# An attention stage whose probabilities and values stay in fp32: one fp32 product in place of three fp16 ones

## The chip, the cores and the metric

The kernel runs on one core of a Trainium2 chip. The metric is the time of one execution on the device in microseconds, the median of several runs. The engines named below are TensorE (PE, with its weight loads as PEld), VectorE (DVE), ScalarE (ACT), GpSimd (POOL) and SyncE (SP), which here issues DMAs.

## The reference, cut to what matters

Three stages follow each other: an attention with a forgetting bias, a mixture of eight experts whose gate is normalised by eight Sinkhorn rounds, and a bilinear layer. The change lies in the attention's last lines.

```
B, H, S, D = 2, 8, 576, 64
scores = q @ k.T / sqrt(D) + min(-(cum[:, None] - cum[None, :]), 0)   # causal
scores = scores - max(scores, -1)
attn = exp(scores)
attn = attn / (sum(attn, -1) + 1e-9)
x = attn @ v                                  # to (1152, 512)
x = sum over e of P[:, e] * (relu(x @ w1[e]) @ w2[e])    # E = 8
out = ((x @ w_a) * (x @ w_b)) @ w_out
```

## The kernel before, in words

The matmuls take fp16, and a matrix that needs more digits is split in two: hi is the fp16 rounding of the scaled fp32 value, lo the fp16 rounding of what hi left out. A product of two such matrices is three fp16 products, hi·hi, hi·lo and lo·hi, summed in fp32 in PSUM.

**Values.** `v_prep(b)` loads one batch of v (five blocks of 128 rows, the last of 64) into a staging buffer, takes a sum of squares on ACT for a power of two as scale, and splits each block into `vs[b]`: hi by ACT or POOL (L358, L362), lo by DVE or POOL (L372, L366 and L367). Each head has 64 hi columns, a column of ones whose product gives the row sum of the probabilities, and 64 lo columns. The staging buffers are `wun` for batch 0 and `stage` for batch 1, which also hold expert 0's weights.

**Probabilities.** The 1152 rows are nine tiles: four of 128 query rows for each batch, and a ninth with the last 64 rows of both. For each tile `row_max` makes scores and reduces them on DVE (`mxr`), `shift` brings the maxima into the transposed queries (`ush`, `ut`), and `probs` makes transposed scores in groups of up to 512 columns in PSUM (`st`). For each group ACT takes the exponential into an fp32 tile `p32` (L894), hi is copied to fp16 into `pt` by ACT, POOL or DVE (L901, L900), and lo is subtracted by POOL or DVE (L904, L903). When all key blocks of a head are there, `pv` multiplies: three matmuls for each key block (L922, L923, L924), with the probabilities as stationary operand, so that each loads 128 query columns (64 in the ninth tile) and streams 65 or 64 columns of values into `xp`. Over both batches these are 160 products of 128 query columns and 80 of 64. `x_tile` divides by the row sum (`rs`, `xb`, L936 to L938), splits the result and transposes it by DMA into `xt`.

**The rest.** Right behind each tile of attention comes expert 0 for that tile (`e0_tile`: gate, h as `mb<-xt,wun`, y as `mb<-wun,h`, with the relu and its split as `h` on ACT and DVE). Its PE instructions stand between those of the attention. After the ninth tile the attention's memory is given back, and experts 1 to 7 and the bilinear layer follow.

**The order of work.** Each instruction is recorded with the engines that could do it, an assumed cost, what it reads and writes, and a rank. A planner lays out the whole program before anything runs: it picks an engine for each instruction and an order for each engine, from the assumed costs. On the chip each engine then takes its instructions strictly in that order. So a change of a cost or of an instruction moves the order on all engines. The three fp16 matmuls of a product are assumed at 93 ns.

Of the kernel before, what the change touches and what calls it, by code (L numbers as in the profile page):

```python
# [246 lines left out]
def forgetting_attention_moe_bilinear_kernel(  # L247
# [14 lines left out]
    nc = tc.nc  # L262
# [110 lines left out]


    XE = 6
    NJ = S // 128
    att = ExitStack()
    ap = att.enter_context(tc.tile_pool(name="att", bufs=1))
# [1 line left out]
    NSS, NST, NP32, NPT, NB3 = 2, 2, 2, 5, 2  # L380
    ka1 = ap.tile([128, H, NT], F16, name="ka1")
    ka2 = ap.tile([128, H, NT], F16, name="ka2")
    vs = [ap.tile([128, NBLK, H, 130], F16, name=f"vs{b}") for b in range(B)]
    kn1 = ap.tile([128, H, 2, D], F16, name="kn1")
    kn2 = ap.tile([128, H, 2, D], F16, name="kn2")
    qa = [ap.tile([128, H, 2, D], F16, name=f"qa{i}") for i in range(2)]
# [2 lines left out]
    b4 = [ap.tile([128, H, 128], F16, name=f"b4_{i}") for i in range(2)]  # L389
    p32 = [ap.tile([128, 512], F32, name=f"p32_{i}") for i in range(NP32)]  # L390
    pts = [ap.tile([128, 2, 512], F16, name=f"pt{i}") for i in range(NPT)]
    xb = ap.tile([128, H, D], F32, name="xb")
    xhl = ap.tile([128, 2, DM], F16, name="xhl")
    raw = ap.tile([128, 6, DM], F32, name="raw")
# [77 lines left out]
    for x, key in ((kn2, ("kn2", 1)), (qa[0], ("qa", 0, 1)), (qa[1], ("qa", 1, 1))):  # L472
        g.add("POOL", 500, lambda x=x: nc.gpsimd.memset(x[:, :, 1], 0.0), w=[key], rank=0.5)
    for b in range(B):
        g.add("POOL", 200, lambda b=b: nc.gpsimd.memset(vs[b][:, :, :, 64:66], 1.0), w=[("vone", b)], rank=0.7)

    def consts_():
        f = sel.rearrange("p h a -> p (h a)")
# [105 lines left out]


    def v_prep(b, rank, rel=0.0):
        if b == 0:
            uf = [units[2 + i].rearrange("p z c f -> p (z c f)").bitcast(F32) for i in range(2)]
            sv = [uf[j // 4][:, (j % 4) * DM:(j % 4 + 1) * DM] for j in range(NBLK)]
            svk = [[("u", 2 + j // 4, (j % 4) // 2, 2 * (j % 2) + y) for y in range(2)] for j in range(NBLK)]  # L590
        else:
            sv = [stage[j // 4][:, (j % 4) * DM:(j % 4 + 1) * DM] for j in range(NBLK)]
            svk = [[("st", j // 4, j % 4)] for j in range(NBLK)]
        mxs = scol(NBLK)
        g.add("DVE", 60, lambda: nc.vector.memset(mxs, 0.0), w=[("vm", b)], rank=0)
        for j in range(NBLK):
            kr = 128 if j < NJ else vrem
            g.add("DMA", 1456 * kr / 128, lambda q, j=j, kr=kr: q.dma_start(
                out=sv[j][0:kr].rearrange("p (h d) -> p h d", h=H),
                in_=v[b, :, j * 128:j * 128 + kr, :].rearrange("h s d -> s h d")), w=svk[j], rank=rank, rel=rel)  # L600
            g.add("ACT", 800, lambda j=j, kr=kr: sumsq(mxs[0:kr, j:j + 1], sv[j][0:kr], junk[0:kr]), r=svk[j] + [("vm", b)], w=[("vmx", b, j)], rank=rank)
        sx, iv = scale_chain(mxs, 13, True, rank, [("vmx", b, j) for j in range(NBLK)], ("vsx", b), root=True)

        def svs():
            nc.vector.tensor_scalar(isx[:, b * NJ:(b + 1) * NJ], iv.to_broadcast([128, NJ]), 2.0 ** (13 - XE), None, op0=ALU.mult)
            nc.vector.tensor_scalar(isx[64 * b:64 * b + 64, 2 * NJ:2 * NJ + 1], iv[64 * b:64 * b + 64], 2.0 ** (13 - XE), None, op0=ALU.mult)

# [26 lines left out]
    def cc(ci, i, r=slice(0, 128)):  # L634
        return cst[r, ci, i:i + 1]
# [215 lines left out]

    stc, ptc, p3c = [0], [0], [0]

    def probs(t, zb, rank):

        z4 = t % 2
# [13 lines left out]
        for gr in groups:  # L870
# [8 lines left out]
            def mm(gr=gr, y=y, bb=bb):  # L879
                for w, (_, h, i) in enumerate(gr):  # L880
# [10 lines left out]
            nl = sum(i == (j if t < 2 * NJ else NJ) for (_, _, i) in gr)  # L891
            g.add("PE", (2 * len(gr) + nl) * pe_n(wd), mm, r=[("b3", zb), ("b4", z4), "idb", "msk"] + [("ka", nm, x) for nm in ("kn1", "kn2") for x in kts],
                  w=[("st", y)], rank=rank)
            g.add("ACT", 280 + n * 0.833, lambda y=y, p3=p3, kr=kr, n=n, bb=bb: nc.scalar.activation(  # L894
                p32[p3][0:kr, 0:n], st[y][0:kr, 0:n], AF.Exp, scale=cc(bb, ESC, slice(0, kr))), r=[("st", y), ("cst", bb)], w=[("p32", p3)], rank=rank)
            hi = pts[pi][0:kr, 0, 0:n]
            lo = pts[pi][0:kr, 1, 0:n]
            src = p32[p3][0:kr, 0:n]
            g.add(("DVE", "POOL", "ACT"), (70 + 0.6 * n, 150 + n, 170 + n * 0.833), (lambda hi=hi, src=src: nc.vector.tensor_copy(hi, src),
                  lambda hi=hi, src=src: nc.gpsimd.tensor_copy(hi, src),  # L900
                  lambda hi=hi, src=src: nc.scalar.activation(hi, src, AF.Copy)), r=[("p32", p3)], w=[("pt", pi, 0)], rank=rank)  # L901
            g.add(("DVE", "POOL"), (130 + 1.04 * n, 150 + 2.2 * n), (
                lambda hi=hi, lo=lo, src=src: nc.vector.tensor_tensor(out=lo, in0=src, in1=hi, op=ALU.subtract),  # L903
                lambda hi=hi, lo=lo, src=src: nc.gpsimd.tensor_tensor(out=lo, in0=src, in1=hi, op=ALU.subtract)),  # L904
                r=[("p32", p3), ("pt", pi, 0)], w=[("pt", pi, 1)], rank=rank)
            for w, blk in enumerate(gr):
                where[blk] = (pi, w)
            for h in range(H):
                mine = [(bb, h, i) for i in (range(j + 1) if t < 2 * NJ else [NJ, *range(NJ)])]
                if (bb, h) in done or not all(x in where for x in mine):  # L910
                    continue
                done.add((bb, h))
                at = [(x[2],) + where[x] for x in mine]

                def pv(h=h, bb=bb, at=at):
                    q0 = 0 if t < 2 * NJ else 64 * bb
                    o = xp[h // 4][q0:q0 + wd, (h % 4) * 65:(h % 4) * 65 + 65]
                    for x, (i, pi_, w) in enumerate(at):
                        kw = kcol(bb, i)[1]
                        ph, pl = (pts[pi_][0:kw, y, w * wd:(w + 1) * wd] for y in range(2))  # L920
                        v1, vl = vs[bb][0:kw, i, h, 0:65], vs[bb][0:kw, i, h, 66:130]
                        nc.tensor.matmul(o, lhsT=ph, rhs=v1, start=(x == 0), stop=False)  # L922
                        nc.tensor.matmul(o[:, 0:64], lhsT=ph, rhs=vl, start=False, stop=False)  # L923
                        nc.tensor.matmul(o, lhsT=pl, rhs=v1, start=False, stop=(x == len(at) - 1))  # L924

                g.add("PE", 93 * len(at), pv, r=[("pt", pi_, y) for (_, pi_, _) in at for y in range(2)] + [("vone", bb)]
                      + [(nm, bb, i) for (i, _, _) in at for nm in ("vs", "vh")], w=[("xp", h // 4)], rank=rank + 1)

    def x_tile(t, rank):
        xf = xb.rearrange("p h d -> p (h d)")  # L930
        hf = xhl.rearrange("p z d -> p (z d)")
        for gg in range(2):
            def f(gg=gg):
                o = xp[gg][:, 0:260].rearrange("p (h d) -> p h d", d=65)
                r4 = rs[:, 4 * gg:4 * gg + 4]
                nc.vector.tensor_scalar(r4, o[:, :, 64], 1e-9 * PSC, 2.0 ** (13 - XE), op0=ALU.add, op1=ALU.mult)  # L936
                nc.vector.reciprocal(r4, r4)
                nc.vector.tensor_tensor(out=xb[:, 4 * gg:4 * gg + 4], in0=o[:, :, 0:64],  # L938
                                        in1=r4.rearrange("p (h o) -> p h o", o=1).to_broadcast([128, 4, D]), op=ALU.mult)

            g.add("DVE", 900, f, w=[("xp", gg), ("xb", gg)], rank=rank)
        xbk = [("xb", 0), ("xb", 1)]
        g.add(("ACT", "POOL", "DVE"), (600, 690, 380), (lambda: nc.scalar.activation(xhl[:, 0], xf, AF.Copy),
              lambda: nc.gpsimd.tensor_copy(xhl[:, 0], xf), lambda: nc.vector.tensor_copy(xhl[:, 0], xf)), r=xbk, w=[("xhl", 0)], rank=rank)
        g.add(("DVE", "POOL"), (663, 1280), (lambda: nc.vector.tensor_tensor(out=xhl[:, 1], in0=xf, in1=xhl[:, 0], op=ALU.subtract),
              lambda: nc.gpsimd.tensor_tensor(out=xhl[:, 1], in0=xf, in1=xhl[:, 0], op=ALU.subtract)), r=[("xhl", 0)], w=xbk + [("xhl", 1)], rank=rank)
        g.add("SP", 1600, lambda: nc.sync.dma_start_transpose(
            out=xt[:, :, :, xc[t]:xc[t] + 128].rearrange("p z c t -> p (z c) t"), in_=hf),
            r=[("xhl", 0), ("xhl", 1)], w=[("xt", t)] + (["ncum", "ntail", "sn"] if t == 0 else []), rank=rank - 5, issue=1300.0)
# [836 lines left out]
```

## Time and profile before

| | us |
|---|---|
| median of 3 runs (1058.57 to 1062.61) | 1058.78 |
| the profiled execution | 1059.17 |
| its span, first to last instruction | 1057.3 |
| PE busy, share of the span | 1008.0 (95%) |
| DVE busy | 720.3 (68%) |
| ACT busy | 517.4 (49%) |
| POOL busy | 156.2 (15%) |

The shares are means over stages that differ. The attention with expert 0 lasts until about 225 us of the span; POOL does nearly all its work there. Matmuls overlap, and the recorded time of one is longer than its distance to the next, so the pace of TensorE is read from the starts of the rows.

### The profile page before, as it was taken

How to read it: one execution, taken by the hardware profiler on the slowest of the kernel's cores; microseconds unless marked ns; L12 is line 12 of the kernel's file. 1: busy time of each engine (PE TensorE's matmuls, PEld its weight loads, DVE VectorE, ACT ScalarE, POOL GpSimd, SP SyncE). 2: the span in 40 equal slices, each digit the busy share in tenths (PEclk: the TensorE clock that was granted, in tenths of full speed). 3: DMA queues.
4: the chain of work that ended last, by engine and by line, in shares of the span. 5: the costliest groups of instructions: out<-in, count | busy, mean ns of one | idle time of the engine just before them, and what ended most of it. 6: DMA issues, size and time to landing. Idle time of an engine off the chain costs nothing.

```text
span 1057.3 us, 18899 instructions
## 1 busy us (share of the span) xinstructions
PE 1008.0 (95%) x7676; PEld 625.6 (59%) x7676; DVE 720.3 (68%) x1488; ACT 517.4 (49%) x970; POOL 156.2 (15%) x190
## 2 busy tenths in 40 slices
PE   1688999999999999999999999999999999999998
PEld 0577777866546745754774674575476464555445
DVE  7986865159975898795789889489768684434201
ACT  5786567346535635653672774455355354343100
POOL 4876755320000000000000000000000000000000
PEclk9989999999999999999999999999999999999999
DMA  9883751021123134423324340431443652300001
GB/s 243 166 201 80 163 79 25 2 75 56 41 80 120 41 122 158 160 81 120 120 81 153 131 155 40 158 122 40 160 160 144 184 121 80 127 34 1 20 31 40
DMA packets 123063, 108.75 MB, mean 103 GB/s; under 512 B 87632, under 2 KB 100176, under 8 KB 119136
## 3 DMA queue, kind: packets, MB, share of 16 engines
q1 hardware_dynamic: 121632, 106.74, 33.9%
q8 instruction: 60, 0.98, 0.4%
q10 hardware_dynamic: 1344, 0.81, 0.3%
q14 instruction: 27, 0.22, 0.1%
HBM read 75.29 MB, written 18.09 MB: 88 GB/s over the span
## 4 chain that ended last, share of the span: by engine, by line
PE 88%; DVE 6%; SPq 2%; DMA 1%; issue 1%; ACT 1%; POOL 1%; DVEq 0%; POOLq 0%; ACTq 0%
PE yb L1048 10%; PE yb L1049 10%; PE yb L1050 10%; PE yb L1400 4%; PE yb L1402 4%; PE yb L1401 4%; PE mb L1400 3%; PE mb L1402 3%; PE mb L1401 3%; PE yb L1656 2%; PE yb L1654 2%; PE yb L1655 2%; PE yb L1584 2%; PE yb L1586 2%; PE yb L1585 2%; PE mb L1584 1%
## 5 line engine op out<-in xcount | busy, mean ns | idle before, releaser
L1048 PE MATMUL yb<-wun,ht 128*128 128x512 f16 x504 | 191.0, 379 | 0.0
L1050 PE MATMUL yb<-wun,ht 128*128 128x512 f16 x504 | 191.0, 379 | 0.0
L1049 PE MATMUL yb<-wun,ht 128*128 128x512 f16 x504 | 191.0, 379 | 0.0
L372 DVE SCALAR_TENSOR_TENSOR wun<-stage,sc,wun 128x1024 f16<-128x1024 f32 (+1 forms) x65 | 78.9, 1236 | 11.6 <-ACT wun L358 11.5
L1050 PEld LDWEIGHTS <-ht 128*128 128x128 f16 x504 | 49.3, 98 | 59.5
L1400 PE MATMUL yb<-sx,wun 128*128 128x288 f16 x288 | 82.3, 286 | 2.0 <-DVE sc L343 1.1
L1458 DVE SCALAR_TENSOR_TENSOR acc<-yb,pe,acc 128x512 f32<-128x512 f32 x63 | 47.3, 750 | 53.7 <-PE yb L1050 52.7
L1049 PEld LDWEIGHTS <-ht 128*128 128x128 f16 x504 | 49.3, 98 | 57.7 <-issue 0.3
L1048 PEld LDWEIGHTS <-ht 128*128 128x128 f16 x504 | 49.3, 98 | 57.6
L1402 PE MATMUL yb<-sx,wun 128*128 128x288 f16 x288 | 82.4, 286 | 0.0
L1401 PE MATMUL yb<-sx,wun 128*128 128x288 f16 x288 | 82.3, 286 | 0.0
L1401 PEld LDWEIGHTS <-wun 128*128 128x128 f16 x672 | 65.7, 98 | 22.3 <-issue 4.0
L1400 PEld LDWEIGHTS <-wun 128*128 128x128 f16 x672 | 65.7, 98 | 18.4
L1402 PEld LDWEIGHTS <-wun 128*128 128x128 f16 x672 | 65.7, 98 | 16.6
L358 ACT ACTIVATE wun<-stage,sc 128x1024 f16<-128x1024 f32 (+1 forms) x60 | 60.9, 1040 | 28.3 <-PE yb L1050 14.0
L355 ACT ACTIVATE jk<-stage 128x1024 f16<-128x1024 f32 x52 | 54.7, 1052 | 35.8 <-DMA stage<-in_moe_w_dram 35.3
L904 POOL TENSOR_TENSOR pt<-p,pt 128x512 f16<-128x512 f32 (+1 forms) x48 | 57.1, 1192 | 31.7 <-ACT pt L901 22.6
L1410 ACT ACTIVATE ht<-yb 128x288 f16<-128x288 f32 x96 | 38.8, 406 | 40.7 <-PE yb L1402 40.1
L1400 PE MATMUL mb<-xt,wun 128*128 128x288 f16 x192 | 54.9, 286 | 0.0
L1401 PE MATMUL mb<-xt,wun 128*128 128x288 f16 x192 | 54.9, 286 | 0.0
L1402 PE MATMUL mb<-xt,wun 128*128 128x288 f16 x192 | 54.9, 286 | 0.0
L1411 DVE SCALAR_TENSOR_TENSOR ht<-yb,ht 128x288 f16<-128x288 f32 x96 | 43.0, 453 | 17.1 <-ACT ht L1410 16.7
(358 smaller groups left out, 2639.3 us busy)
## 6 DMA issues: line engine op xcount, KB each, us to landing
stage<-in_moe_w_dram SPq DMA_DIRECT2D x26, 1024.0 KB, 5.3
md<-wun SPq DMA_DIRECT2D x15, 1024.0 KB, 3.9
wun<-md SPq DMA_DIRECT2D x11, 1024.0 KB, 5.0
mr<-in_moe_w_a_dram SPq DMA_DIRECT2D x12, 512.0 KB, 5.8
mr<-in_moe_w_b_dram SPq DMA_DIRECT2D x12, 512.0 KB, 3.9
mr<-in_moe_w_out_dram SPq DMA_DIRECT2D x6, 1024.0 KB, 4.9
stage<-in_moe_w_dram SPq DMA_DIRECT2D x22, 256.0 KB, 4.0
stage<-md SPq DMA_DIRECT2D x4, 1024.0 KB, 4.8
```

What stands on the lines that cost most here:

```text
L355: nc.scalar.activation(out, src, AF.Square, accum_out=dst)
L358: nc.scalar.activation(hi, src, AF.Copy, scale=scale)
L372: eng.scalar_tensor_tensor(out=lo, in0=src, scalar=scale, in1=hi, op0=ALU.mult, op1=ALU.subtract)
L904: lambda hi=hi, lo=lo, src=src: nc.gpsimd.tensor_tensor(out=lo, in0=src, in1=hi, op=ALU.subtract)),
L1048: nc.tensor.matmul(pp, lhsT=hh, rhs=wh, start=(f == 0), stop=False)
L1049: nc.tensor.matmul(pp, lhsT=hh, rhs=wl, start=False, stop=False)
L1050: nc.tensor.matmul(pp, lhsT=hl, rhs=wh, start=False, stop=(f == KF - 1))
L1400: nc.tensor.matmul(p, lhsT=wh, rhs=xh, start=first and ch == 0, stop=False, skip_group_check=True)
L1401: nc.tensor.matmul(p, lhsT=wh, rhs=xl, start=False, stop=False, skip_group_check=True)
L1402: nc.tensor.matmul(p, lhsT=wl, rhs=xh, start=False, stop=ch == 1, skip_group_check=True)
L1411: g.add("DVE", 160 + 1.04 * CN, lambda: nc.vector.scalar_tensor_tensor(out=hl(), in0=src(), scalar=0.0, in1=hh(), op0=ALU.max, op1=ALU.sub ...
L1458: g.add("DVE", 663, lambda t=t, z=z: nc.vector.scalar_tensor_tensor(out=acc[:, t], in0=yb[z], scalar=pe[:, t, e:e + 1], in1=acc[:, t], op0 ...
```

## The change

Both batches are in `FV`, the list of batches whose probabilities and values stay in fp32. v is loaded straight into `vs[b]`, now an fp32 tile of 65 columns for each head (the 64 values and the ones); its splits are gone, and the sum of squares is kept, since its scale still sets that of the output. The exponential is written in fp32 straight into the memory of `pt` (`ptf` is that memory seen as fp32); the hi copy and the lo subtraction are gone. One fp32 matmul takes the place of three fp16 ones, with an assumed cost of 125 ns. The scale of v, which was multiplied into hi and lo, is now applied in `x_tile` through `isx`, and for the ninth tile through a new column `xs8` that is put together by one POOL memset and two small DVE copies.

```diff
+    FV = (0, 1)
-    vs = [ap.tile([128, NBLK, H, 130], F16, name=f"vs{b}") for b in range(B)]
+    vs = [ap.tile([128, NBLK, H, 65], F32, name=f"vs{b}") if b in FV else ap.tile([128, NBLK, H, 130], F16, name=f"vs{b}") for b in range(B)]
+    ptf = [x.rearrange("p z n -> p (z n)").bitcast(F32) for x in pts]
+    xs8 = scol()
...
     def v_prep(b, rank, rel=0.0):
-        if b == 0:
+        if b in FV:
+            sv = [vs[b][:, j, :, 0:64] for j in range(NBLK)]
+            svk = [[("vs", b, j)] for j in range(NBLK)]
+        elif b == 0:
...
+        if b in FV:
+            g.add("DVE", 70, lambda: nc.vector.tensor_copy(xs8[64 * b:64 * b + 64], isx[64 * b:64 * b + 64, 2 * NJ:2 * NJ + 1]),
+                  r=[("isx", b)], w=["xs8"], rank=rank + 0.6)
+            return
...
+            if bb in FV:
+                g.add("ACT", 280 + n * 0.833, lambda y=y, pi=pi, kr=kr, n=n, bb=bb: nc.scalar.activation(
+                    ptf[pi][0:kr, 0:n], st[y][0:kr, 0:n], AF.Exp, scale=cc(bb, ESC, slice(0, kr))),
+                    r=[("st", y), ("cst", bb)], w=[("pt", pi, 0), ("pt", pi, 1)], rank=rank)
+            else:
+                split_p(y, pi, p3, kr, n, bb, rank)
...
+                        if bb in FV:
+                            nc.tensor.matmul(o, lhsT=ptf[pi_][0:kw, w * wd:(w + 1) * wd], rhs=vs[bb][0:kw, i, h], start=(x == 0), stop=(x == len(at) - 1))
+                            continue
...
-                g.add("PE", 93 * len(at), pv, r=[("pt", pi_, y) for (_, pi_, _) in at for y in range(2)] + [("vone", bb)]
+                g.add("PE", (125 if bb in FV else 93) * len(at), pv, r=[("pt", pi_, y) for (_, pi_, _) in at for y in range(2)] + [("vone", bb)]
...
+        rsc = xs8 if t == 2 * NJ else isx[:, t:t + 1] if t // NJ in FV else 2.0 ** (13 - XE)
...
-                nc.vector.tensor_scalar(r4, o[:, :, 64], 1e-9 * PSC, 2.0 ** (13 - XE), op0=ALU.add, op1=ALU.mult)
+                nc.vector.tensor_scalar(r4, o[:, :, 64], 1e-9 * PSC, rsc, op0=ALU.add, op1=ALU.mult)
```

The first products of the first tile on PE, before: `xp` is the output, `vs` the values, `pt` the probabilities.

```order
L922 LDWEIGHTS pt_107
L922 MATMUL xp_136<-vs_94,pt_107 128x65
L923 LDWEIGHTS pt_107
L923 MATMUL xp_136<-vs_94,pt_107 128x64
L924 LDWEIGHTS pt_107
L924 MATMUL xp_136<-vs_94,pt_107 128x65
```

The same place now, with the two matmuls before it and the next tile's transpose behind it; an fp32 matmul stands here as one row, its weight loads within it.

```order
L912 LDWEIGHTS ka_92
L912 MATMUL st_135<-b_0_103,ka_92 128x128
L914 LDWEIGHTS idb
L914 MATMUL st_135<-msk_131,idb 128x128
L941 MATMUL xp_136<-vs_94,pt_107 128x65 x4
L941 MATMUL xp_137<-vs_94,pt_108 128x65 x4
L857 LDWEIGHTS ut_122
L857 MATMUL ss_133<-id_129,ut_122 128x128
```

All eight heads of the tile now stand together behind the last scores, and each has one matmul where it had three.

DVE before, from the second lo split of batch 0's values to the first tile's shift (`vs<-wun` are those splits, `mxr` the row maxima, `ush` and `ut` the shift).

```order
L372 SCALAR_TENSOR_TENSOR vs_94<-wun_77,sc,vs_94 128x8x64 x2
L521 TENSOR_REDUCE sc<-mb_84 1x1
L372 SCALAR_TENSOR_TENSOR vs_94<-wun_78,sc,vs_94 64x8x64
L795 TENSOR_REDUCE mxr<-ss_132 128x4
L795 TENSOR_REDUCE mxr<-ss_133 128x4
L334 TENSOR_SCALAR sc<-mb_84 128x1
L838 TENSOR_SCALAR ush<-mxr,cst 128x8
```

DVE now at the same place (`wun<-stage` are lo splits of expert 0's first weights, `kn` a lo split of the keys).

```order
L525 TENSOR_REDUCE sc<-mb_84 1x1
L372 SCALAR_TENSOR_TENSOR wun_75<-stage_73,sc,wun_75 128x512 x2
L372 SCALAR_TENSOR_TENSOR wun_76<-stage_74,sc,wun_76 128x512
L807 TENSOR_REDUCE mxr<-ss_132 128x4
L807 TENSOR_REDUCE mxr<-ss_133 128x4
L372 SCALAR_TENSOR_TENSOR wun_75<-stage_73,sc,wun_75 128x512
L372 SCALAR_TENSOR_TENSOR kn_96<-acc,cst,kn_97 128x8x64
L850 TENSOR_SCALAR ush<-mxr,cst 128x8
```

The place of the values' splits ahead of the first row maxima is taken by splits of weights, and two more splits stand between the maxima and the shift.

## Rows read from the trace of the kernel before

**Rows 1.** Windows of all engines: busy us (instructions) for PE, PEld, DVE, ACT, POOL; clock, DMA, GB/s.

```profile
25.00:50.00 25.00, 14.68 (x113) 11.74 (x114) 24.56 (x50) 17.30 (x34) 22.56 (x23) 1.00 0.84 169
50.00:150.00 100.00, 90.86 (x1275) 73.53 (x1274) 74.54 (x160) 68.11 (x130) 67.79 (x76) 0.95 0.66 138
150.00:225.00 75.00, 74.63 (x1263) 59.36 (x1261) 24.42 (x55) 42.92 (x78) 29.26 (x25) 1.00 0.13 20
225.00:300.00 75.00, 73.33 (x421) 41.41 (x422) 71.56 (x177) 37.28 (x63) 8.16 (x8) 1.00 0.16 57
```

**Rows 2.** The same windows for L922 alone, one matmul of each product.

```profile
25.00:50.00 25.00, 1.57 (x8) 1.04 (x8) 1.00 0.84 169
50.00:150.00 100.00, 11.83 (x96) 9.40 (x96) 0.95 0.66 138
150.00:225.00 75.00, 17.70 (x136) 13.10 (x136) 1.00 0.13 20
```

**Rows 3.** Waits of PE from 25 to 150 us: total us, times, longest.

```profile
PE xp L924 <- POOL pt L904: 2.9, 1, 2.9
...
PE ss L845 <- DVE ut L840: 1.5, 3, 0.8
...
PE mb L1048 <- DVE h L1035: 1.3, 1, 1.3
PE xp L924 <- DVE pt L903: 1.2, 1, 1.2
```

**Rows 4.** Timeline of DVE around 110 us: start, us, line, operation.

```profile
109.62 2.27 DVE L372 SCALAR_TENSOR_TENSOR vs<-stage,sc,vs 128x512 f16<-128x512 f32 x2
111.81 0.68 DVE L1035 SCALAR_TENSOR_TENSOR h<-mb,h 128x512 f16<-128x512 f32 x1
...
113.61 1.29 DVE L372 SCALAR_TENSOR_TENSOR vs<-stage,sc,vs 128x512 f16<-128x512 f32 x1
```

**Rows 5.** What wrote `pt`: count, min/median/max ns, first and last start.

```profile
L904 POOL TENSOR_TENSOR pt<-p,pt x48: 1148/1157/1641, 43.7 to 198.5; 128x512 f16<-128x512 f32 x46, 64x512 f16<-64x512 f32 x2
L901 ACT ACTIVATE pt<-p x44: 629/630/632, 38.2 to 197.7; 128x512 f16<-128x512 f32 x42, 64x512 f16<-64x512 f32 x2
```

**Rows 6.** Timeline of PE: four products of 128 columns, first and following instruction.

```profile
175.72 0.19 PE L922 MATMUL xp<-vs,pt 128*128 128x65 f16 x1
...
176.09 0.22 PE L845 MATMUL ss<-id,ut 128*128 128x128 f16 x1
```

**Rows 7.** Weight loads by shape, to 300 us: count, busy us, mean ns.

```profile
L922 PEld LDWEIGHTS <-pt 128*128 128x128 f16 x160 | 15.6, 101 | 1.6 <-issue 0.7
...
L922 PEld LDWEIGHTS <-pt 128*64 128x64 f16 x64 | 6.3, 110 | 0.7
...
L1175 PEld LDWEIGHTS yb<-pe,ones 128*128 128x128 f32 x16 | 2.8, 190 | 0.6
...
L922 PEld LDWEIGHTS <-pt 64*64 64x64 f16 x16 | 1.6, 103 | 1.3 <-issue 0.4
...
L520 PEld LDWEIGHTS mb<-id,sc 128*1 128x1 f32 x6 | 0.5, 81 | 11.7 <-DVE sc L502 9.6 <-DVE sc L334 2.1
```

**Rows 8.** Timeline of PE: nine fp32 matmuls of 8 columns in a row.

```profile
9.10 1.02 PE L453 MATMUL mb<-id,xt 8*128 8x8 f32 x8 [9.10 <-POOL id masks.py:199]
9.97 0.25 PE L455 MATMUL mb<-id,xt 8*128 8x8 f32 x1
```

**Rows 9.** Timeline of PE: one fp32 product of 72 columns between fp16 ones.

```profile
241.07 0.33 PE L1007 MATMUL mb<-xt,wun 128*128 128x384 f16 x1
241.23 0.34 PE L1175 MATMUL yb<-pe,ones 128*128 128x72 f32 x2
241.40 0.33 PE L1005 MATMUL mb<-xt,wun 128*128 128x384 f16 x1
```

**Rows 10.** Timeline of PE: the ninth tile, first matmuls of two heads.

```profile
184.04 0.21 PE L922 MATMUL xp<-vs,pt 64*64 64x65 f16 x1
...
184.75 0.21 PE L922 MATMUL xp<-vs,pt 64*64 64x65 f16 x1
```

More of the change, by code (lines that the diff above doesn't have):

```diff
@@ L474, in forgetting_attention_moe_bilinear_kernel @@
     for b in range(B):
-        g.add("POOL", 200, lambda b=b: nc.gpsimd.memset(vs[b][:, :, :, 64:66], 1.0), w=[("vone", b)], rank=0.7)
+        g.add("POOL", 200, lambda b=b: nc.gpsimd.memset(vs[b][:, :, :, 64:65] if b in FV else vs[b][:, :, :, 64:66], 1.0), w=[("vone", b)], rank=0.7)
+    g.add("POOL", 100, lambda: nc.gpsimd.memset(xs8, 2.0 ** (13 - XE)), w=["xs8"], rank=0.7)
     def consts_():
@@ L598, in v_prep @@
             g.add("DMA", 1456 * kr / 128, lambda q, j=j, kr=kr: q.dma_start(
-                out=sv[j][0:kr].rearrange("p (h d) -> p h d", h=H),
+                out=sv[j][0:kr] if b in FV else sv[j][0:kr].rearrange("p (h d) -> p h d", h=H),
                 in_=v[b, :, j * 128:j * 128 + kr, :].rearrange("h s d -> s h d")), w=svk[j], rank=rank, rel=rel)
-            g.add("ACT", 800, lambda j=j, kr=kr: sumsq(mxs[0:kr, j:j + 1], sv[j][0:kr], junk[0:kr]), r=svk[j] + [("vm", b)], w=[("vmx", b, j)], rank=rank)
+            g.add("ACT", 800, lambda j=j, kr=kr: sumsq(mxs[0:kr, j:j + 1], sv[j][0:kr], junk[0:kr].rearrange("p (h d) -> p h d", h=H) if b in FV else junk[0:kr]),
+                  r=svk[j] + [("vm", b)], w=[("vmx", b, j)], rank=rank)
         sx, iv = scale_chain(mxs, 13, True, rank, [("vmx", b, j) for j in range(NBLK)], ("vsx", b), root=True)
@@ L852, in forgetting_attention_moe_bilinear_kernel, with split_p @@
     stc, ptc, p3c = [0], [0], [0]
+    def split_p(y, pi, p3, kr, n, bb, rank):
+        g.add("ACT", 280 + n * 0.833, lambda: nc.scalar.activation(
+            p32[p3][0:kr, 0:n], st[y][0:kr, 0:n], AF.Exp, scale=cc(bb, ESC, slice(0, kr))), r=[("st", y), ("cst", bb)], w=[("p32", p3)], rank=rank)
+        hi = pts[pi][0:kr, 0, 0:n]
+        lo = pts[pi][0:kr, 1, 0:n]
+        src = p32[p3][0:kr, 0:n]
+        g.add(("DVE", "POOL", "ACT"), (70 + 0.6 * n, 150 + n, 170 + n * 0.833), (lambda hi=hi, src=src: nc.vector.tensor_copy(hi, src),
+              lambda hi=hi, src=src: nc.gpsimd.tensor_copy(hi, src),
+              lambda hi=hi, src=src: nc.scalar.activation(hi, src, AF.Copy)), r=[("p32", p3)], w=[("pt", pi, 0)], rank=rank)
+        g.add(("DVE", "POOL"), (130 + 1.04 * n, 150 + 2.2 * n), (
+            lambda hi=hi, lo=lo, src=src: nc.vector.tensor_tensor(out=lo, in0=src, in1=hi, op=ALU.subtract),
+            lambda hi=hi, lo=lo, src=src: nc.gpsimd.tensor_tensor(out=lo, in0=src, in1=hi, op=ALU.subtract)),
+            r=[("p32", p3), ("pt", pi, 0)], w=[("pt", pi, 1)], rank=rank)
     def probs(t, zb, rank):
@@ L893, in probs @@
                   w=[("st", y)], rank=rank)
[L894 to L905, printed above, removed]
+            if bb in FV:
[4 more added lines that the diff above has]
+                split_p(y, pi, p3, kr, n, bb, rank)
             for w, blk in enumerate(gr):
@@ L930, in x_tile @@
         xf = xb.rearrange("p h d -> p (h d)")
+        rsc = xs8 if t == 2 * NJ else isx[:, t:t + 1] if t // NJ in FV else 2.0 ** (13 - XE)
+        rk = ["xs8"] if t == 2 * NJ else [("isx", t // NJ)] if t // NJ in FV else []
         hf = xhl.rearrange("p z d -> p (z d)")
@@ L939, in f @@
                                         in1=r4.rearrange("p (h o) -> p h o", o=1).to_broadcast([128, 4, D]), op=ALU.mult)
-            g.add("DVE", 900, f, w=[("xp", gg), ("xb", gg)], rank=rank)
+            g.add("DVE", 900, f, r=rk, w=[("xp", gg), ("xb", gg)], rank=rank)
         xbk = [("xb", 0), ("xb", 1)]
```

## The prediction

> **What bounds the kernel now.** I read the windows first. From 150 to 225 us TensorE is busy 74.6 of 75 us, behind that 73.3 of 75; from 50 to 150 it is busy 90.9 of 100, from 25 to 50 only 14.7 of 25 [rows 1]. The reader is to see two regimes within the attention. Up to about 50 us a chain over several engines sets the pace, with DVE at 24.6 and POOL at 22.6 of 25 us; from 150 us on TensorE alone does, and DVE is down at 24.4 of 75. Between them TensorE is nearly full and stops now and then. So time added to TensorE behind 150 us is paid in full, time added before 50 us can vanish in its 10.3 us of idle, and work taken from DVE, ACT and POOL is worth only what TensorE waits for. The waits come next: the attention's second product waited 2.9 us for a lo on POOL and 1.2 us for one on DVE, y of expert 0 waited 1.3 us for an h on DVE, a shift 0.8 us [rows 3]. Last come the timelines of TensorE, for the price of a product in either type.
>
> **Taken away.** 48 lo subtractions of about 1.16 us on POOL and 44 hi copies of 0.63 us on ACT, some 56 and 28 us of engine time [rows 5], with the splits of both batches' values (about 1.1 us each on DVE, [rows 4]). That is a lot of engine time, but POOL's and ACT's share of it behind 150 us lies beside a full TensorE and is worth nothing. What it is worth is the waits it ends. The two waits for a lo go: 2.9 + 1.2 = 4.1 us. Two lo splits of values (2.27 us) stand on DVE right ahead of the h that y waited 1.3 us for, and a third (1.29 us) ahead of the shift that TensorE waited 0.8 us for [rows 3, 4]. Together 6.2 us by name. What is next late there is the same DVE with its row maxima and splits of weights: the order shows three splits of weights ahead of the first row maxima, where the splits of values stood, and two more splits before the shift. So I count nothing for the start before the first scores.
>
> The loads of v go to another tile and no split waits for them; the scale of v is now needed only where a tile's output is divided, far later. The four small new instructions (a memset, two copies of one column, a scale read from a column) cost DVE well under 1 us in all; they lie beside TensorE's work, and if that cover were gone they would cost just that. The division's new wait for the scale ends early: batch 1's splits already use theirs at 109.6 us [rows 4], and the ninth tile's products begin at 184.0 [rows 10].
>
> **Added: the fp32 products.** Today four products of 128 query columns, twelve matmuls, run from 175.72 to 176.09 [rows 6]: 31 ns a matmul, 93 ns a product. No product of this kind in fp32 stands in the trace, so I bound it by its nearest rows.
>
> An fp32 product runs as two passes: the gate's normalisation issues 8 products and shows 16 loads [rows 7] and the timeline x2 [rows 9]. A load of 128 fp32 columns is recorded at 190 ns, one of a single fp32 column at 81, one of 128 fp16 columns at 101 [rows 7]. So the fp32 load grows by about 109 ns over 127 columns, and fp16 loads of 128 columns hardly more than that of one fp32 column. Nine fp32 matmuls that stream only 8 columns each start from 9.10 to 9.97 [rows 8], that is 8 distances in 0.87 us: 109 ns each, although there is almost nothing to stream. They are held by the load. In the third place a whole product of 72 columns lies between fp16 matmuls: from 241.23 to 241.40, 170 ns [rows 9]. Its first load began under the matmul ahead (160 ns long), so 170 is one load that shows, 109, and one stream of 72 columns, about 60. All three agree that one load runs under one matmul, and no second one ahead of it.
>
> In a run of products each matmul streams for less than the next load takes. A pass then costs 109 ns and a product 218, against 93 now: 125 ns more. The lower bound is a load wholly hidden: a pass of about 60 ns, its stream, and a product of 120. The upper bound is a product whose streams are not hidden either, 2 x 170 = 340. I take 218, because nine matmuls in a row show that pace. 160 products [rows 7] x 125 ns = 20.0 us. The first load of a run lies partly under the matmul before it and the last stream comes behind its load; these two about cancel.
>
> The ninth tile has 80 products of 64 query columns (64 + 16 loads, [rows 7]), in 16 heads of five; a head takes 0.71 us from its start to the next [rows 10], of which 15 matmuls at 31 ns are 0.47. An fp32 load of 64 columns is in no row; between 81 ns for 1 column and 190 for 128 a straight line makes its growth about 55 ns, under a stream of about 57. Ten passes of 57 are 0.57, 0.10 more for a head, 1.6 us in all. If such a load took 109 as well, it would be 0.62 for a head and 9.9 us.
>
> The Trainium skill, in TensorE: Matmul & The Clock Gate, LDWEIGHTS (loading the stationary operand), gives a load as its columns over 1.2 per ns: 107 ns for 128, which this trace bears out for fp32, and 53 ns for 64, which no row here shows for fp32. By it the ninth tile would add the same 1.6 us. For fp16 the trace does not follow it: loads of 64 columns go at 31 ns a matmul in the ninth tile's heads.
>
> **The sum.** Added: 20.0 + 1.6 = 21.6 us of TensorE. By windows about 8 of the 160 products fall before 50 us, 96 between 50 and 150, the rest behind [rows 2]: 1.0, 12.0 and 7.0 us, and the ninth tile's 1.6 behind 150. Given back: 6.2 us of named waits. TensorE's idle from 25 to 150 us is 10.3 + 9.1 = 19.5 us [rows 1]; 13.3 of it is left after these. In the middle window, where TensorE has 12 us more to do, the other engines gain time on it and some of the rest must close; at the start the chain stays. I take 30% of 13.3, 4.1 us, with none and all as bounds. 21.6 - 6.2 - 4.1 = 11.3 us slower. The profiled execution took 1059.17, 0.4 above the median of the runs; 1059.2 + 11.3 - 0.4 = 1070.
>
> **The rivals.**
> 1. The loads overlap with the matmuls of the run after all, and a pass of `pv` costs its stream of 60 ns, a product 120: 160 x 27 ns + 1.6 = 5.9 us added, 5.9 - 10.3 = -4.4, 1054.4 us, so not slower. It happens in `pv` alone, and the sign turns at a product of 93 ns + 8.7 us/160, about 147 ns. For it: the recorded load of 190 ns is mostly latency, and a queue can hide that. Against it: the product between fp16 matmuls took 170, and nine loads in a row paid 109 each [rows 8, 9]. The Trainium skill, in FP8 and Floating Point Precision, TensorE Precision Notes, says that true fp32 takes four passes through the array. Read as four fp16 passes at this trace's 31 ns it gives 124 ns a product and about this rival's time. The trace agrees with it for the streams (72 columns in about 60 ns, in each of two passes), and the loads are what it leaves out.
> 2. Little comes back. The planner assumed 125 ns; if TensorE is late by 93 ns a product, DVE stands longer at the division that needs `xp`, and the row maxima of the next tile are queued behind it. Then only the 4.1 us of waits for a lo return, or not even those: 17.5 to 21.6 us slower, 1076 to 1080. For it: DVE has no slack before 50 us. Against it: it has 25 of 100 us between 50 and 150 [rows 1].
> 3. All idle closes: 21.6 - 19.5 = 2.1, 1060.5 us. For it: POOL and ACT lose the longest step between scores and product. Against it: the start depends on loads, row maxima and transposes that stay.
> 4. An fp32 product is lowered to four loads instead of two: 4 x 109 = 436 ns, 343 x 160 = 55 us, about 1100 us. The gate's rows speak against it.
>
> **How the numbers follow.** My forecast has 0.50, rival 1 0.10, rival 2 0.23, rival 3 0.14, rival 4 0.02, something else that makes it faster 0.01. The forecast's own range is 1065 to 1075. The range for 8 in 10 goes from 1057 to 1081: it takes in rivals 2 and 3 and most of the ninth tile's upper bound (1070 + 8.3 = 1078), and leaves out most of rival 1 and all of 4. A measurement can tell about 0.5%, 5.3 us, from no change: within 1053.5 to 1064.1 lie rival 3 and more than half of rival 1, 0.20 together; faster 0.04; slower 0.76.
>
> **What would show it.** In the new profile `pv` has two loads and two matmuls for each product, 480 of each; their loads have a mean near 190 ns, and in a run of products the starts of matmuls lie 0.11 us apart for 128 query columns, 0.06 for 64. TensorE has no wait for a lo left. The end of the attention, now at about 225 us, comes near 236, and everything behind it keeps its length. DVE, ACT and POOL are busy less in sum. The prediction is wrong if matmuls in a run start 0.06 us apart (rival 1), if the attention ends before 228 us (rival 3), or if the time behind the attention changes by more than 2 us.

## The result, and the profile after

The changed kernel takes 1073.51 us (median of four runs, 1072.16 to 1074.31) against 1060.2 for the kernel before (four runs; the forecast started from the median of three, 1058.78): a ratio of 1.0126, with a 95% interval of 1.010 to 1.0153. That is 13.3 us slower; the forecast was 11.3 us slower, 1070 in a range of 1057 to 1081. The profiled execution took 1074.31 us, its span is 1072.2, 14.9 more than before.

The windows of the kernel after, same columns as [rows 1]:

```profile
25.00:50.00 25.00, 13.97 (x115) 11.96 (x116) 20.13 (x46) 16.02 (x34) 16.62 (x20) 1.00 0.91 181
50.00:150.00 100.00, 94.48 (x1130) 78.97 (x1128) 58.75 (x155) 51.26 (x100) 31.29 (x43) 0.98 0.68 136
150.00:225.00 75.00, 75.00 (x991) 60.76 (x989) 20.11 (x48) 24.06 (x39) 3.46 (x3) 1.00 0.11 16
225.00:240.00 15.00, 14.06 (x181) 10.87 (x179) 3.49 (x8) 7.99 (x21) 0.00 (x0) 1.00 0.10 19
240.00:300.00 60.00, 58.86 (x353) 34.80 (x353) 56.63 (x154) 34.15 (x60) 8.16 (x8) 1.00 0.22 71
```

The engines that split are relieved: POOL falls from 67.8 to 31.3 us between 50 and 150, DVE from 74.5 to 58.8. TensorE is no less full there: 94.5 of 100 us against 90.9, and still only 14.0 of 25 before 50 us. Its idle from 25 to 150 us goes from 19.5 to 16.5 us, 3 us less where I had forecast 10.3.

The groups of `pv` (line 941), one for each shape; under PE the matmuls, under PEld their loads. They answer to [rows 7]:

```profile
L941 PE MATMUL xp<-vs,pt 128*128 128x65 f32 x320 | 40.5, 276 | 0.0
L941 PE MATMUL xp<-vs,pt 128*64 128x65 f32 x128 | 10.9, 228 | 0.0
L941 PE MATMUL xp<-vs,pt 64*64 64x65 f32 x32 | 5.2, 243 | 0.0
L941 PEld LDWEIGHTS xp<-vs,pt 128*128 128x128 f32 x320 | 38.5, 194 | 1.0
L941 PEld LDWEIGHTS xp<-vs,pt 128*64 128x64 f32 x128 | 8.7, 137 | 1.1
L941 PEld LDWEIGHTS xp<-vs,pt 64*64 64x64 f32 x32 | 3.0, 131 | 0.9
```

Two passes for each of 240 products, and loads of 194 ns. The pace stands in TensorE's timeline (start, duration, instruction), which answers to [rows 6] and, with its last two rows, to [rows 10]:

```profile
170.60 0.22 PE L914 MATMUL st<-msk,idb 128*128 128x128 f16 x1
170.65 1.95 PE L941 MATMUL xp<-vs,pt 128*128 128x65 f32 x16
172.44 0.22 PE L911 MATMUL st<-b,ka 128*128 128x128 f16 x1
...
196.97 1.80 PE L941 MATMUL xp<-vs,pt 64*64 64x65 f32 x20
198.70 0.20 PE L911 MATMUL st<-b,ka 128*128 128x64 f16 x1
```

Sixteen passes of 128 query columns take 172.44 - 170.65 = 1.79 us, 112 ns each, 224 a product; 31 ns a matmul and 93 a product before. In the ninth tile twenty passes, two heads, take 1.73 us, 0.87 a head where it was 0.71.

The waits of TensorE from 25 to 150 us, to be held against [rows 3]:

```profile
PE ss L857 <- DVE ut L852: 6.9, 1, 6.9
PE mb L1075 <- DVE h L1060: 2.8, 1, 2.8
PE st L911 <- ACT pt L921: 1.2, 1, 1.2
PE mb L1073 <- DVE h L1060: 1.1, 1, 1.1
```

No wait for a `lo` is left, and the 0.8 us for the shift is gone. The 1.3 us for `h` is not: the same matmul of the same tile (L1048 before, L1073 now) still waits 1.1 us, at 114.3 us. The splits of values no longer stand ahead of that `h` on DVE, but the splits that stand there now wait themselves, for POOL and for a DMA:

```profile
112.37 0.75 DVE L372 SCALAR_TENSOR_TENSOR kn<-acc,cst,kn 128x512 f16<-128x512 f32 x1 [2.07 <-POOL kn L362]
114.06 0.75 DVE L372 SCALAR_TENSOR_TENSOR qb<-raw,cst,qa 128x512 f16<-128x512 f32 x1 [0.94 <-DMA b<-qb]
114.73 0.68 DVE L1060 SCALAR_TENSOR_TENSOR h<-mb,h 128x512 f16<-128x512 f32 x1
```

What fell most is a kind of wait that [rows 3] leave out. For a scale, TensorE transposes a column of maxima, waits for DVE to reduce it and sends the result back to all rows (`mb` and `sc` in the rows). In the same window its waits for DVE in these come to 9.4 us before:

```profile
PE mb L522 <- DVE sc L521: 4.2, 3, 2.1
PE mb L520 <- DVE sc L502: 3.2, 2, 2.9
PE mb L520 <- DVE sc L334: 2.0, 1, 2.0
```

and to 3.0 after:

```profile
PE mb L524 <- DVE sc L506: 1.7, 1, 1.7
PE mb L526 <- DVE sc L525: 1.1, 3, 0.4
PE mb L524 <- DVE sc L334: 0.2, 1, 0.2
```

The waits that grew are those for another `h`, 2.8 us, and, the longest, for the first shift, 6.9 us. DVE's timeline shows why the shift is late:

```profile
28.49 2.96 DVE L372 SCALAR_TENSOR_TENSOR wun<-stage,sc,wun 128x512 f16<-128x512 f32 x3 [0.60 <-ACT wun L358]
31.38 1.28 DVE L807 TENSOR_REDUCE mxr<-ss 128x4 f32<-128x512 f32 x2
32.58 1.10 DVE L372 SCALAR_TENSOR_TENSOR wun<-stage,sc,wun 128x512 f16<-128x512 f32 x1
33.60 1.64 DVE L372 SCALAR_TENSOR_TENSOR kn<-acc,cst,kn 128x512 f16<-128x512 f32 x1
35.16 0.66 DVE L850 TENSOR_SCALAR ush<-mxr,cst 128x8 f32<-128x8 f32 x1
...
36.05 1.00 DVE L852 TENSOR_TENSOR ut<-ush,ut 128x8 f16<-128x8 f32 x1
```

Three splits of expert 0's weights stand ahead of the first row maxima, and two more splits before the shift: what the prediction had read from the order.

**An account of TensorE.** To see where the 14.9 us went I added up, for each matmul from the trace, the time from its start to its end or to the next start, whichever comes first; what is left over is idle. The sum runs from TensorE's first matmul (at 9 us) to the Sinkhorn normalisation's first transpose (234.7 us before, 249.0 after); "behind" is from there to TensorE's last matmul. All in us, of the profiled execution, with its mean granted clock; the time is the median of the runs, beside which the kernel before took 1059.8 to 1061.1 in the later comparisons. The profiled execution is one run and can lie off the median: with 8 columns it took 1074.5.

| kernel | time | `pv` | other matmuls | idle | behind | clock |
|---|---|---|---|---|---|---|
| before | 1060.2 | 28.8 | 162.6 | 34.2 | 819.5 | 0.995 |
| after | 1073.5 | 50.0 | 158.5 | 31.1 | 820.1 | 0.998 |
| three fp16 halves | 1055.4 | 27.9 | 156.9 | 35.7 | 821.9 | 1.000 |
| batch 1 alone | 1069.3 | 40.2 | 159.1 | 37.1 | 820.7 | 0.993 |
| batch 0 alone | 1060.1 | 38.6 | 156.8 | 31.3 | 819.3 | 1.000 |
| plan with 93 ns | 1069.8 | 50.0 | 156.5 | 31.1 | 818.1 | 1.000 |
| plan with 224 ns | 1068.2 | 50.7 | 158.1 | 26.2 | 818.1 | 0.997 |
| plan with 340 ns | 1072.0 | 52.8 | 159.5 | 27.9 | 818.4 | 0.998 |
| 8 columns | 1080.3 | 50.7 | 163.0 | 28.2 | 818.0 | 0.990 |
| start moved | 1070.0 | 49.9 | 157.2 | 29.5 | 818.0 | 0.997 |
| start, 224 ns | 1067.3 | 51.7 | 158.0 | 25.9 | 818.0 | 1.000 |
| batch 0, 224 ns | 1060.7 | 38.9 | 155.9 | 32.1 | 819.1 | 1.000 |
| before, start moved | 1058.6 | 28.3 | 161.4 | 35.0 | 819.1 | 0.994 |
| batch 0, start moved | 1057.3 | 39.8 | 158.5 | 26.1 | 819.4 | 0.995 |

From before to after: `pv` +21.3, other matmuls -4.1, idle -3.2, behind +0.6, 14.6 of the 14.9 us.

### The profile page after: what moved, and what is told of

It is laid out like the page before. It is cut to its first block, busy times and chain, and to the rows that moved or that the text cites. A ratio compares the mean times of both kernels' runs of the same rounds, so it can differ in the third digit from the quotient of the medians.

```text
span 1072.2 us, 18248 instructions
## 1 busy us (share of the span) xinstructions
PE 1025.0 (96%) x7436; PEld 643.3 (60%) x7436; DVE 698.3 (65%) x1476; ACT 487.2 (45%) x920; POOL 87.5 (8%) x133
## 4 chain that ended last, share of the span: by engine, by line
PE 90%; DVE 4%; SPq 2%; ACT 2%; DMA 1%; issue 1%; POOL 0%; DVEq 0%; ACTq 0%
PE yb L1073 10%; PE yb L1075 10%; PE yb L1074 10%; PE xp L941 4%; PE yb L1425 4%; PE yb L1427 4%; PE yb L1426 4%; PE mb L1425 3%; PE mb L1426 3%; PE mb L1427 3%; PE yb L1681 2%; PE yb L1679 2%; PE yb L1680 2%; PE yb L1609 2%; PE yb L1610 2%; PE yb L1611 2%
## 5 line engine op out<-in xcount | busy, mean ns | idle before, releaser
L1073 PE MATMUL yb<-wun,ht 128*128 128x512 f16 x504 | 191.0, 379 | 0.0
L372 DVE SCALAR_TENSOR_TENSOR wun<-stage,sc,wun 128x1024 f16<-128x1024 f32 (+1 forms) x64 | 78.0, 1242 | 11.3 <-ACT wun L358 11.3
L1073 PEld LDWEIGHTS <-ht 128*128 128x128 f16 x504 | 49.4, 98 | 57.5
L941 PE MATMUL xp<-vs,pt 128*128 128x65 f32 (+2 forms) x480 | 54.8, 261 | 0.0
L1436 DVE SCALAR_TENSOR_TENSOR ht<-yb,ht 128x288 f16<-128x288 f32 x96 | 43.0, 454 | 16.5 <-ACT ht L1435 16.2
```

Of the source, the lines that this page charges most:

```text
L372: eng.scalar_tensor_tensor(out=lo, in0=src, scalar=scale, in1=hi, op0=ALU.mult, op1=ALU.subtract)
L941: nc.tensor.matmul(o, lhsT=ptf[pi_][0:kw, w * wd:(w + 1) * wd], rhs=vs[bb][0:kw, i, h], start=(x == 0), stop=(x == len(at) - 1))
L1073: nc.tensor.matmul(pp, lhsT=hh, rhs=wh, start=(f == 0), stop=False)
L1436: g.add("DVE", 160 + 1.04 * CN, lambda: nc.vector.scalar_tensor_tensor(out=hl(), in0=src(), scalar=0.0, in1=hh(), op0=ALU.max, op1=ALU.sub ...
```

## The experiments

Four theories. First: the price of the fp32 product, set by its loads, is what the change costs, and about 7 us come back. Second: the plan was made for 125 ns a product, and an order made for the true price would return several us. Third: the new wait at the start is what was lost. Fourth, formed after the first four runs: any change of the plan's costs draws another order, and orders differ by some us whatever they were made for.

**Three fp16 products on the upper halves.**

```diff
-nc.tensor.matmul(o, lhsT=ptf[pi_][0:kw, ...], rhs=vs[bb][0:kw, i, h], ...)
+ph = ptf[pi_].bitcast(F16)[0:kw, 2 * w * wd + 1:2 * (w + 1) * wd:2]
+vh = vs[bb][0:kw, i, h].bitcast(F16)[:, 1::2]
+for y in range(3):
+    nc.tensor.matmul(o, lhsT=ph, rhs=vh, ...)
```

> The changed kernel, with its plan and its order, but each fp32 product is computed by three fp16 matmuls on the upper halves of the same probabilities and values; what the lower halves carry is left out. If the price of the fp32 product is what the change costs (first theory), pv falls from 50.0 us of TensorE to about 29 and the time by 21 us less what then comes back as idle, at most the 7.3 us that the change had given back: 1053 to 1060, and the better half of that if the removal of the splits is a gain of its own (1053). If the order is what costs (second theory: a plan made for 125 ns a product, with weight splits ahead of the first row maxima), the order stays and so do its waits: 1060 or more, with the wait of 6.9 us for ut at 30 us still there.

Measured: 1055.42 us (12 runs) against 1060.03, ratio 0.9955 (0.9937 to 0.9974). The product is all that differs from the kernel after, and the order, with its long wait, stayed:

```profile
L944 PE MATMUL xp<-vs,pt 128*128 128x65 f16 x480 | 20.3, 195 | 0.4 <-ACT pt L921 0.4
L944 PEld LDWEIGHTS <-pt 128*128 128x128 f16 x480 | 18.2, 98 | 1.7 <-ACT pt L921 0.5
```

```profile
PE ss L857 <- DVE ut L852: 6.8, 1, 6.8
```

`pv` fell by 22.1 us and the time by 18.1, with idle up 4.6. The kernel leaves out what the lower halves carry, so it is a test and not a version. The product's price is more than the whole loss, and all the rest of the change is a gain of 4.6 us. With the same long wait this kernel is faster than before.

**One batch alone**, `FV = (1,)` and `FV = (0,)`:

```diff
-    FV = (0, 1)
+    FV = (1,)
```

> fp32 products for batch 1 alone, batch 0 as before. Batch 1 has 80 of the 160 products: 80 x 131 ns = 10.5 us, and 40 of the ninth tile's, 0.2. First theory: TensorE is nearly full where batch 1 runs, little comes back (1 to 3 us of waits for a lo): 1068 to 1070. If the two halves cost alike, half of 13.3 us: 1067. If the start is what costs (third theory), the values of batch 0 are split as before and the start stays as before: about 1060 + 10.5 - 7 = 1064.

> fp32 products for batch 0 alone, batch 1 as before. The same 10.7 us of TensorE. First theory: they fall where TensorE still waits, so more comes back, 4 to 6 us: 1065 to 1067, and with batch 1 alone the two add up to the whole change (13.3 us). Third theory: the new wait of 6.9 us at 30 us comes with the values of batch 0 and is most of the loss: 1068 or more, and batch 1 alone near 1064.

Measured: batch 1 alone 1069.31 us, ratio 1.0081 (1.0053 to 1.0109); batch 0 alone 1060.1, ratio 0.9992 (0.9975 to 1.0009). Batch 1 came as the first theory had it. Batch 0 did not: it costs 9.9 us of `pv` and nothing in time. The account says what paid for it: 2.9 us less idle and 5.8 us less in the other matmuls. Most of the latter goes with the granted clock. Two windows of the kernel before (columns as in the first fence; the third figure from the end is the clock):

```profile
70.00:80.00 10.00, 10.00 (x113) 8.34 (x110) 8.96 (x10) 8.35 (x17) 9.57 (x9) 0.74 0.63 140
...
100.00:110.00 10.00, 8.17 (x135) 8.03 (x132) 7.86 (x29) 2.99 (x6) 5.71 (x9) 0.83 0.79 140
```

The same with batch 0 alone in fp32:

```profile
70.00:80.00 10.00, 10.00 (x131) 8.58 (x130) 8.23 (x13) 8.19 (x18) 8.70 (x9) 1.00 0.57 128
...
100.00:110.00 10.00, 10.00 (x152) 9.90 (x152) 7.57 (x25) 5.50 (x10) 5.70 (x8) 1.00 1.01 166
```

Before, TensorE runs part of these stretches at the lower of its two levels, 1.2 GHz: from 68.4 to 75.2 us and from 102.5 to 105.9, 10.2 us in all. The fp16 passes of `pv` are 55 ns apart there, 29 to 33 elsewhere, so this costs up to 5.1 us. With batch 0 alone in fp32 the clock is full all through. Each of the two falls comes at the end of a wait of TensorE for a scale, 2.1 us at 66.7 and 1.8 at 100.8; with batch 0 alone no wait between 50 and 110 us is longer than 1.1 us. Whether the clock stayed up because these waits went or because of the fp32 passes, no run took apart; with the start moved (below) batch 0 in fp32 too runs 10.2 us at the lower level, from 40.5 us, behind a wait of 3.4. The third theory loses here: the same wait of 6.9 us stands in batch 0 alone (6.86 at 30.4 us), which costs nothing, and batch 1 alone waits 6.2 us for its shift there too. The two halves add up to 9.4 us and not to 13.3.

**The plan's price.** In the kernel after:

```diff
-g.add("PE", (125 if bb in FV else 93) * len(at), pv, ...
+g.add("PE", (224 if wd == 128 else 120) * len(at), pv, ...
```

and in two more runs `93` and `(340 if wd == 128 else 180)`.

> The changed kernel, but its planner is told what a product takes, 224 ns of 128 query columns and 120 of 64, in place of 125. Second theory (the order made for 125 ns holds TensorE up): the 3 us that came back less than forecast return, 1068 to 1071. First theory: TensorE has the same work and is full from 50 us on, so within 2 us of the changed kernel, 1072 to 1075.

> Both batches in fp32, the planner told 93 ns a product, further from the truth than 125. If it is the true price that gave back 5.3 us with 224 ns (second theory), a worse one costs more: 1074 to 1077. If plans differ among themselves by some us whatever price they were made for (fourth theory: the order is a draw, the price of 50 us of pv is not), anywhere from 1067 to 1076, and pv stays at 50 to 51 us.

> Both batches in fp32, the planner told 340 and 180 ns, half too much. Second theory: worse than at 224 (1068.2), 1069 to 1072, since an order that waits for TensorE too long leaves it idle. Fourth theory: anywhere from 1067 to 1076, with pv again at 50 to 51 us of TensorE and the difference in idle and in stretches at the lower clock.

Measured: 1068.22 us with 224 ns (ratio 1.0077, 1.0047 to 1.0106; one of its seven runs took 1074.95), 1069.81 with 93 (1.0084, 1.0063 to 1.0104), 1072.03 with 340 (1.0099, 1.0074 to 1.0124), and 1073.51 with 125. After the first of them the second theory looked right: 5.3 us came back, and idle was 4.9 us less. The other two speak against it. A price that is more wrong, 93, does nearly as well by time as the true one, so the truth of the price is not needed to get the time back. `pv` takes 50 to 53 us in all four. The fourth theory stands: four orders of the same work lie within 5.3 us, and the order that the change happened to get has the highest median, though its runs touch those with 340 (up to 1072.83). By place the second theory is not wholly out: idle is less with 224 and 340 (26.2 and 27.9 us) and not with 93 (31.1), whose gain stands in the other matmuls and behind, 2.0 us each.

**Eight columns in place of 65.**

```diff
-nc.tensor.matmul(o, lhsT=..., rhs=vs[bb][0:kw, i, h], ...)
+c0 = 0 if x == 0 else 57
+nc.tensor.matmul(o[:, c0:65], lhsT=..., rhs=vs[bb][0:kw, i, h, c0:65], ...)
```

> The changed kernel, but of every head's products only the first streams 65 columns of values; the others stream the last 8 (the columns before are left out of their sums). Loads are as in the changed kernel. If the load of 128 fp32 columns holds a pass (first theory), the passes stay at 109 to 112 ns apart and the time at 1073 (1071 to 1075). If the stream does (an fp32 pass that is slow by itself), a pass of 8 columns falls from 112 ns to about 15 to 60, and pv by 10 to 15 us: 1059 to 1065.

Measured: 1080.34 us, ratio 1.0203 (1.0175 to 1.0231). Groups and timeline of `pv`:

```profile
L942 PE MATMUL xp<-vs,pt 128*128 128x8 f32 x192 | 27.4, 251 | 0.0
L942 PE MATMUL xp<-vs,pt 128*128 128x65 f32 x128 | 23.3, 281 | 0.0
L942 PEld LDWEIGHTS xp<-vs,pt 128*128 128x128 f32 x320 | 38.6, 194 | 1.0
```

```profile
154.31 2.12 PE L942 MATMUL xp<-vs,pt 128*128 128x65 f32 x18
156.29 0.38 PE L803 MATMUL ss<-ka,b 128*128 128x512 f16 x1
```

Eighteen passes, twelve of them of 8 columns, take 1.98 us: 110 ns each, as with 65 columns, and `pv` is 50.7 us against 50.0. The load holds the pace, shown directly. What neither theory expected is that the median rose; that is below.

**The start.** Expert 0's first `lo` splits may start only at the plan's 37 us; the same edit in four kernels.

```diff
-                      w=[("u", un, 1, cc) ...] + [("st", z, cc) ...], rank=srank)
+                      w=[...], rank=srank, rel=RL if name == 1 and e == 0 else 0.0)
+RL = 37e3
```

> The changed kernel, but the plan lets the lo splits of expert 0's first weights start only at its 37 us, so that the first row maxima and the first shift come ahead of them on DVE. Third theory (the new wait of 6.9 us for ut at 30 us is what the changed kernel lacks to the forecast): that wait shrinks to 2 to 3 us and 3 to 5 us return, 1068 to 1070. First theory, now with the run of batch 0 alone, which has the same wait and still costs nothing: what is moved at the start comes back as later waits for the same splits, within 2 us, 1071 to 1075.

> Both batches in fp32, the planner told 224 and 120 ns, and the lo splits of expert 0's first weights held to 37 us. If what is moved at the start comes back later, 1067 to 1070, as without the move (1068.2). If the start is a loss of its own, 1063 to 1066.

> The kernel before, three fp16 products and all splits, with the lo splits of expert 0's first weights held to 37 us as in the run on the start. It tells how far a small change of the plan moves the kernel before. If the gain of 3.5 us there was the start's (third theory), the same start gives 2 to 4 us here, 1056 to 1058, and would beat both kernels. Fourth theory: within 5 us of 1060 on either side; the splits of values stand ahead of the first row maxima here, and what is held back comes later on a DVE without slack, so rather 1060 to 1064.

> fp32 products for batch 0 alone, with the lo splits of expert 0's first weights held to 37 us: the candidate for a version that beats both. Third theory: 3 to 5 us less than batch 0 alone (1060.1), 1055 to 1057. Fourth theory: batch 0 alone already runs at the full clock all through and its idle behind 50 us is 7.5 us, so no plan has much to gain: 1058 to 1062.

Measured: in the kernel after 1069.97 us (ratio 1.0096, 1.0075 to 1.0118); with 224 ns 1067.34 (1.0068, 1.0049 to 1.0087); in the kernel before 1058.64 (0.9978, 0.9964 to 0.9991); with batch 0 alone 1057.28 (0.9966, 0.9952 to 0.9979). That is 3.5, 0.9, 2.4 and 2.8 us less than without the move, so by size the third theory's 2 to 5 us came three times of four, though only the first time lies in the range written down for it (1068 to 1070). By the place they did not. In the kernel after the one wait became two:

```profile
PE ss L857 <- DVE ut L852: 4.3, 1, 4.3
PE ss L857 <- DVE rs L961: 2.5, 1, 2.5
```

and its idle is 1.6 us less, the other matmuls 1.3, the stretch behind 2.1. In the kernel before idle is even 0.8 us up. Only with batch 0 alone does the start itself gain, since there two row maxima and the shift come first on DVE:

```profile
28.42 0.69 DVE L807 TENSOR_REDUCE mxr<-ss 128x4 f32<-128x512 f32 x1 [0.24 <-PE ss L788]
29.28 0.69 DVE L807 TENSOR_REDUCE mxr<-ss 128x4 f32<-128x512 f32 x1 [0.16 <-PE ss L788]
...
31.03 0.62 DVE L852 TENSOR_TENSOR ut<-ush,ut 128x8 f16<-128x8 f32 x1
```

There the shift is done at 31.7 us (37.1 in the kernel after), and against batch 0 alone idle falls by 5.2 us, of which 2.9 are lost again in `pv` and the other matmuls, at a granted clock of 0.995 against 1.000. Nor is it a loss that the change made, since the kernel before gains from the move too. This version beats both kernels, the one before by 0.34%: less than the 0.5% that the prediction set as a bound, but its interval does not reach 1. Most of that is the move and not the fp32 product: the kernel before with the same move took 1058.64, 1.4 us more in the same comparison, and the runs of the two overlap (1056.63 to 1059.54 and 1056.30 to 1060.22).

**Batch 0 alone with the true price.**

> fp32 products for batch 0 alone, and the planner is told 224 and 120 ns for them. If the true price gives the plan back idle as it did for both batches (5.3 us, of which the larger part lay before 110 us, where batch 0 runs), 1060.1 - 3 to 5 = 1055 to 1057, faster than both kernels. If batch 0 alone has nothing left to give (its idle from 50 us on is 7.5 us in all), 1059 to 1061.

Measured: 1060.7 us, ratio 1.0014 (0.9999 to 1.0028). Nothing came back, one more point against the second theory.

## Why the prediction was right

**The price.** Forecast 20.0 us for the products of 128 columns and 1.6 for the ninth tile, 21.6; the account shows 18.7 and 2.6, 21.3. A pass costs 112 ns where the nine matmuls of the gate gave 109 [rows 8], and eight streamed columns cost as much as 65. By the account a product of 128 columns rose by 117 ns, from 110 to 227, and not by 125: before, not every pass went at 31 ns. The ninth tile is the worse estimate: its passes of 128 rows and 64 columns do go at 58 ns, as forecast, but two of 64 x 64 are 108 ns apart, and from those to the others and back it takes 148 and 151 ns, 120 and 124 before. The Trainium skill, in TensorE: Matmul & The Clock Gate, LDWEIGHTS (loading the stationary operand), gives a load as its columns over 1.2 per ns, by estimate 107 and 53 ns for 128 and 64 columns: the pace in the trace agrees for the first two shapes (112 and 58) and not for 64 x 64 (108). Where the Trainium skill, in FP8 and Floating Point Precision, TensorE Precision Notes, names four passes for true fp32, these runs show two pairs of load and matmul for each product. Three slips of the working change the forecast by less than 0.5 us: 30% of 13.3 is 4.0 and not 4.1, rival 3 comes to 1060.9 and not 1060.5, and a stream of 65 columns is 54 ns by the row's 60 for 72, not 57.

**What comes back.** Forecast 10.3 us, all of it idle. By the account 3.2 us of idle came back and 4.1 in other matmuls. Here a step failed: "Together 6.2 us by name" was taken as a gain. Of the named waits those for a `lo` and for the shift went, 4.9 us, and that for `h` stayed at 1.1 of its 1.3; then waits of the same size came up, the 6.9 us for the first shift and 2.8 for another `h`. A wait that is removed is worth its length only if nothing stands right behind it; here DVE had weight splits there (five of them, 73.3 to 80.2 us, ahead of that `h`) or a split that itself waits. What did give TensorE time was not in the list: the waits for scales, 6.4 us less. "At the start the chain stays" held: idle from 25 to 50 us was 10.3 and is 11.0 [rows 1]. What I had not in the sum is the granted clock: in the attention the lower level stands for 10.2 us before and for 3.4 after (81.8 to 85.2, behind the wait of 2.8), so up to 3.4 of the 4.1 us are that. The rest I leave open. What the clock is worth in time no run isolates: batch 1 alone took 1068.5 and 1068.7 in its two runs at 1.000 and 1071.1 and 1071.3 in the two at 0.993, but batch 0 with the start moved took longest, 1059.54, in its one run at 1.000.

**What lies behind** the attention was to keep its length within 2 us: the attention ends at 238.8 us (224.5 before; 236 forecast), and the stretch from the Sinkhorn on differs by 0.6 us.

**The rivals.** Rivals 1 and 4 are out by the passes, 224 ns a product and not 120 or 436, and rival 3 by the idle that stays. Rival 2 came close: 4.1 us of idle that return against 3.2 measured, and its 1076 is nearer to 1073.5 than 1070 is. DVE does stand longer at the division (27.9 us in 13 waits for `pv`, 17.5 in 8 before), but with the plans of 93 and 224 ns it stands longer still (42.6 and 38.2 us) and both are faster, so its reason falls.

So the forecast's 1070 came from a right price and from a give-back 2.3 to 3.9 us too large (8.0 by the medians, 6.4 by the profiled executions), in part for another reason than the one given. By idle alone, as the prediction had it, 18 us would have been lost, rival 2's figure; that the other matmuls gave back 4.1 us was not foreseen, and that the total comes out near the forecast is in part luck.

## What to carry to other kernels

An fp32 product in place of three fp16 ones is priced by its loads in these runs: two loads of as many columns as the stationary side has, 112 ns each at 128, with 8 or 65 columns streamed; three fp16 matmuls of 65 columns are cheaper, 93 ns against 224. It cost nothing in batch 0, where TensorE had idle time and stretches at the lower clock, and in batch 1, where TensorE is nearly full, 9.3 us of the 11.4 that it added to `pv`. Before a loss of some us is put down to a wait or to a planner's cost, run the same work in two or three other orders: here these alone differed by 5.3 us.

## What the hardware showed unexpectedly

Streaming less went with a slower kernel. With 8 columns, the same plan and the same order as after, the median is 6.8 us higher, and the granted clock is lower in each of its four runs: 1074.5 us at 0.990, 1079.25 and 1081.43 at 0.986, 1084.5 at 0.984, where all four runs of the kernel after had 0.998. The profiled run is the fastest of the four and no slower than the kernel after: `pv` takes 0.7 us more and the other matmuls 163.0 us against 158.5, while idle is 2.9 and the stretch behind 2.1 us less. In it the lower level stands in three stretches of the attention, 69.9 to 76.7, 199.6 to 203.0 and 206.4 to 216.6 us, 20.5 us in all, against one of 3.4 in the kernel after. TensorE is not idle in any of them:

```profile
70.00:80.00 10.00, 10.00 (x79) 8.18 (x79) 7.73 (x11) 6.97 (x15) 7.96 (x8) 0.67 0.51 104
...
199.60:203.00 3.40, 3.40 (x50) 3.40 (x48) 0.28 (x1) 0.08 (x1) 0.00 (x0) 0.50 0.00 0
...
206.40:216.60 10.20, 10.20 (x89) 9.70 (x88) 1.52 (x4) 0.60 (x1) 0.00 (x0) 0.50 0.00 0
```

Passes of 64 query columns are 107 ns apart there in place of 58. Nor is TensorE idle in the 7 us before each of these falls, while in the other kernels every fall in the attention came at most 2 us behind a wait of TensorE of 0.7 us or more (and not every such wait was followed by one). So a pass that waits for its load counts as busy in the profile, and here the kernel that streamed fewer columns had the lower clock. Why, and whether the 6.8 us are the clock's alone, no run took apart.
